# Query-key-normed attention with a gated MLP on one core: a slot's scores, values and sums in one visit of TensorE's small tiles

## The chip, the cores and the metric

The kernel runs on one NeuronCore of a Trainium2 chip. Its engines are TensorE (PE in the profile; PEld is its weight load), VectorE (DVE), ScalarE (ACT), GpSimd (POOL) and the queue that starts transfers (SP). The metric is the device time of one execution in microseconds (us).

## The reference

Attention with normed queries and keys, then a two-layer MLP whose activation is h - tanh(h). All is float32.

```python
batch, n_heads, seq, head_dim = (8, 12, 448, 64)     # d_model 768, d_ff 2048
q_n, k_n = (rmsnorm(q, g_q), rmsnorm(k, g_k))
scores = scale * np.matmul(q_n, k_n.transpose(0, 1, 3, 2))
attn = np.exp(scores - max) / sum
x = np.matmul(attn, v)            # then (batch * seq, heads * head_dim)
h = x @ w_in
out = (h - np.tanh(h)) @ w_out
```

## The kernel before

**Slots.** The attention is cut into 48 slots: 8 batches by 6 pairs of heads. A slot `s` works on 448 queries and 448 keys of two heads. The keys are cut into three chunks of 128 and a last one of 64. For each chunk `scores` (L438) makes the transposed scores, keys on the partitions and queries along the row, for the two heads in two PSUM banks, and an exponential of ScalarE (L443) for each head reads them and writes `p`. Head 0 sits on partitions 0 to 63 and head 1 on 64 to 127, so its two matmuls use the upper and lower half of TensorE's array at once ("64\*128" in the profile). A float32 matmul is two instructions; the profile counts instructions.

- `last_values` (L477) and `values` (L489) multiply the exponentials by V, in tiles of 32 columns, four side by side.
- `totals` (L510) sums the exponentials over the keys by a matmul with ones, also in tiles of 32 columns, and VectorE takes the reciprocal (L515).
- `divide` (L523) multiplies the values by it on VectorE, and the result is `xT`, the MLP's input. For the upper three pairs of heads of a batch it is followed by four sums on GpSimd (`tt`, L537 to L540).
- `turn` transposes queries and keys two slots ahead (L411, L415). `squares`, `norm` (VectorE L129, L130; GpSimd's power L131) and `norm_q` (L400) make the norms three slots ahead. `add` and `add_last` (L459, L460, L467) add up the exponentials on VectorE, so that `totals` has one matmul to do in place of four.

Scores run one slot ahead: in slot `s` the values of `s` are made from exponentials that slot `s - 1` left, and the scores of `s + 1` are made.

**The MLP as a stream.** The MLP of batch `b - 1` runs beside the attention of batch `b`. It is a Python generator, `mlp`, whose matmuls (L578) use the full 128\*128 array. `run(gap)` takes matmuls from it until their time, counted in a fixed figure per matmul, has reached the sum of the gaps asked for. From the third batch on a slot holds four gaps, and a gap is 14 matmuls, 28 instructions. Both layers use products of seven (a Strassen form): per set the order is 1, 5, 6, 2, 3, 7, 4. The hidden layer has four sets of 42 matmuls, three slots; the projection three sets of 56, three slots. What VectorE, ScalarE and GpSimd do behind each product (`use`, L615 to L659, `store`) is issued where the product ends or one product later (`late["todo"]`). In the hidden layer each set ends with `factors`: two sums on VectorE (L625, L626), one on GpSimd (L627).

**The order.** The order of the program is written by hand, and each engine takes its instructions in that order. A slot before is: scores 0 and 1 of the next slot; a gap; `turn`; a gap; the last chunk's scores; `last_values`, `totals`, `values`, `divide`; scores 2; then `add`, `add_last`, `norm` and `norm_q`, each behind half a gap. So TensorE is twice in a slot on small tiles (a visit): once for scores 0 and 1, once from the last chunk's scores to scores 2.

**PSUM.** Of eight banks, three (`mm`) belong to the MLP and five (`sc`) to the attention, and both are dealt out in turn:

```python
banks = {name: [ps.tile([P, 512], F32, name=f"{name}{i}") for i in range(n)] for name, n in (("sc", 5), ("mm", 3))}
def bank_of(name):
    turns[name] += 1
    return banks[name][turns[name] % len(banks[name])]
```

A slot takes 13 turns of the five: six for scores 0 to 2, two for the last chunk, one for the sums, two for the values, two for `turn`. A matmul into a bank waits until the last reader of the bank's previous content is done.

The first batch's slots (`first_slot`) have no MLP beside them and issue scores 2 of one slot and scores 0 and 1 of the following one with no other TensorE work between.

Of the kernel before, what the change touches and what calls it, by code (L numbers as in the profile page):

```python
# [133 lines left out]
def bounded_path(tc, ctx, q, k, v, moe_w_in, moe_w_out, out, g_col, ident, ones, half_ones, neg_half, early):  # L134
# [22 lines left out]
    NP = H // 2  # L157
# [46 lines left out]
    def load(s, names):  # L204
        b, hp = steps[s]
        for name in names:
            src = {"q": q, "k": k, "v": v}[name]
            if s == 0 and name != "v":
                t = early[name]
            else:  # L210
                shape = [CP, 2, NCH, D] if name == "q" else [P, NCH, 2, D] if name == "k" else [P, 2, NCH, D]
                t = nat.tile(shape, F32, name=f"{name}_nat", bufs=3 if name == "v" else 2)
                fetch(nc, name, t, src[b, 2 * hp : 2 * hp + 2])
            loaded[name, s] = t
# [191 lines left out]
    def turn(s, tk, tq):  # L406

        rr, n = normed.pop(s), early["n"]
        kn = loaded.pop(("k", s))
        for c in range(NCH):  # L410
            nc.tensor.transpose(tk[:, c * P : (c + 1) * P], kn[:, c].rearrange("p h d -> p (h d)"), ident)  # L411
        kT = qkp.tile([P, S], F32, name="kT")
        nc.scalar.mul(kT, tk[:, :S], g_col)
        for c in range(NCH):
            nc.tensor.transpose(  # L415
                tq[:, c * CP : (c + 1) * CP], n[:, c].rearrange("p h d -> p (h d)"), ident[:CP, :CP]
            )
        qT = qkp.tile([P, S], F32, name="qT")
        nc.scalar.copy(out=qT, in_=tq[:, :S])
        turned[s] = rr, kT, qT  # L420

    def sc_bank():
        return bank_of("sc")

    def scores(s, c):

        rr, kT, qT = turned[s]
        halves, keys, n = (1, P, S) if c < KF else (2, KR, HS)
        name, bufs = ("p", 2) if c < 2 else ("p_full", 1) if c < KF else ("p_last", 2)
        if c == 1:  # L430
            p = probs[s, 1] = probs[s, 0]
        else:
            p = probs[s, c] = pp.tile([P, 2, 2 if c < 2 else 1, n], F32, name=name, bufs=bufs)
        tiles = [sc_bank() for _ in range(2)]
        for i in range(halves):
            for h in range(2):
                r = slice(h * D, (h + 1) * D)
                nc.tensor.matmul(  # L438
                    tiles[h][i * keys : (i + 1) * keys, :n], lhsT=kT[r, c * P : c * P + keys],
                    rhs=qT[r, i * n : (i + 1) * n], start=True, stop=True,  # L440
                )
        for h in range(2):
            nc.scalar.activation(  # L443
                p[:, h, c if c < 2 else 0, :], tiles[h][:, :n], AF.Exp, scale=rr[:, 0, 2 * c + h : 2 * c + h + 1]
            )
# [5 lines left out]
    def add(s):  # L451

        if s <= NP + NP // 2:
            sums[s] = []
            return
        t = early["sum"]
        sums[s] = [t]
        p = full(s)
        nc.vector.tensor_tensor(out=t, in0=p[0], in1=p[1], op=ALU.add)  # L459
        nc.vector.tensor_tensor(out=t, in0=t, in1=p[2], op=ALU.add)  # L460
# [8 lines left out]
    def last_values(s, av):  # L469

        v_nat, p = loaded["v", s], probs[s, KF]
        for n in range(2):
            keys = slice(n * KR, (n + 1) * KR)
            for m in range(2):
                for h in range(2):
                    r = (2 * m + h) * BL
                    nc.tensor.matmul(  # L477
                        av[n][r : r + BL, :HS], lhsT=v_nat[keys, h, KF, m * BL : (m + 1) * BL],
                        rhs=p[keys, h, 0], start=True, stop=False,
                    )  # L480

    def values(s, av):
        v_nat, p = loaded.pop(("v", s)), full(s)
        for n in range(2):
            for c in range(KF):
                for m in range(2):
                    for h in range(2):
                        r = (2 * m + h) * BL
                        nc.tensor.matmul(  # L489
                            av[n][r : r + BL, :HS], lhsT=v_nat[:, h, c, m * BL : (m + 1) * BL],  # L490
                            rhs=p[c][:, h, n * HS : (n + 1) * HS], start=False, stop=(c == KF - 1),
                        )
        return av

    def totals(s, dn):

        parts = [t[:, h, n * HS : (n + 1) * HS] for t in sums.get(s, ()) for n in range(2) for h in range(2)]
        parts = [(parts, [ones[:, :BL]] * 2)] if parts else []
        if not sums.pop(s):
            for p in full(s):  # L500
                parts.append(
                    ([p[:, h, n * HS : (n + 1) * HS] for n in range(2) for h in range(2)], [ones[:, :BL]] * 2)
                )
            last = probs[s, KF]
            parts.append(([last[:, h, 0] for _ in range(2) for h in range(2)], [half_ones[:, n] for n in range(2)]))
        for i, (moving, by) in enumerate(parts):
            for n in range(2):
                for h in range(2):
                    r = (2 * n + h) * BL
                    nc.tensor.matmul(  # L510
                        dn[r : r + BL, :HS], lhsT=by[n], rhs=moving[2 * n + h],
                        start=(i == 0), stop=(i == len(parts) - 1),
                    )
        rs = whole[s] = sp.tile([P, HS], F32, name="rs")
        nc.vector.reciprocal(rs, dn[:, :HS])  # L515

    def divide(s, av):
        b, hp = steps[s]
        rs = whole.pop(s)
        x = xT[b, hp] = xp.tile([P, S], F32, name="xT")  # L520
        for n in range(2):
            for m in range(2):
                nc.vector.tensor_tensor(  # L523
                    out=x[m * D : (m + 1) * D, n * HS : (n + 1) * HS],
                    in0=av[n][m * D : (m + 1) * D, :HS], in1=rs[n * D : (n + 1) * D], op=ALU.mult,
                )
        for c in range(NCH):
            del probs[s, c]
        if hp < HC:
            return  # L530
        c = hp - HC
        if c == 0:
            tt[b] = tp.tile([P, 3, HC, HS], F32, name="tt", bufs=1)
        eng = nc.vector if b == 0 and c == HC - 1 else nc.gpsimd
        x11, x12, x21, x22 = (xT[b, r][:, n : n + HS] for r in (c, hp) for n in (0, HS))
        t1, t2, t4 = (tt[b][:, i, c] for i in range(3))
        eng.tensor_tensor(out=t1, in0=x12, in1=x11, op=ALU.subtract)  # L537
        eng.tensor_tensor(out=t2, in0=x22, in1=t1, op=ALU.subtract)  # L538
        eng.tensor_tensor(out=x12, in0=x22, in1=x12, op=ALU.subtract)
        eng.tensor_tensor(out=t4, in0=x21, in1=t2, op=ALU.subtract)  # L540
# [225 lines left out]
    def run(ns):  # L766

        spent[1] += ns
        while spent[0] + 1.0 < spent[1]:
            took = next(stream, None)  # L770
            if took is None:
                return
            spent[0] += took
# [4 lines left out]
    def gap_ns(s):  # L778

        if s < 2 * NP:  # L780
            return H_NS / 12 if s % NP < 3 else 4 * S / ENGINE_NS * CD * CF / 12
        return (H_NS + O_NS) / (4 * NP)

    def has(s):
        return 0 <= s < NS
# [32 lines left out]
        weight(EARLY * (s + 3) // (NP + 2))  # L818
        combine(2)

    def slot(s):
        gap = gap_ns(s)
        if s < 2 * NP:
            totals(s, sc_bank())
        if has(s + 1):
            scores(s + 1, 0)
            scores(s + 1, 1)
        if has(s + 2):
            load(s + 2, "v")
        run(gap)  # L830
        if has(s + 2):
            turn(s + 2, sc_bank(), sc_bank())
        if has(s + 3):
            squares(s + 3)
        if has(s + 4):
            load(s + 4, "qk")
        run(gap)
        if has(s + 1):
            scores(s + 1, KF)
        dn = sc_bank() if s >= 2 * NP else None  # L840
        av = [sc_bank() for _ in range(2)]
        last_values(s, av)
        if s >= 2 * NP:
            totals(s, dn)
        divide(s, values(s, av))
        if has(s + 1):
            scores(s + 1, 2)
        for work, n in ((add, 1), (add_last, 1), (norm, 3), (norm_q, 3)):
            run(gap / 2)
            if has(s + n):  # L850
                work(s + n)

    load(0, "qk")
    load(1, "qk")
    weight_load(0)
# [1 line left out]
    for s in range(-3, NP):  # L857
        first_slot(s)
    for s in range(NP, NS):
        slot(s)  # L860
    run(1e9)


# [343 lines left out]
```

## Time and profile before

Three runs gave 1463.94, 1464.91 and 1466.45 us; the median is 1464.91.

| engine | busy us | share of the span |
|---|---|---|
| TensorE, matmuls | 1429.9 | 98% |
| TensorE, weight loads | 1187.1 | 81% |
| VectorE | 818.6 | 56% |
| GpSimd | 512.0 | 35% |
| ScalarE | 456.7 | 31% |

The MLP's matmuls (L578) make up 64% of the chain that ended last, the scores (L438) 9%, the values (L489) 6%. From the third batch on a slot takes 28.94 us. In the timeline a line gives start, length, engine, source line, operation, output and inputs, shape and count; in brackets stand the idle time before it and what ended it. "issue" there means that no awaited engine is seen.

### The profile page before, as it was taken

The page shows a single profiled execution, that of the slowest core. Times are in us where ns is not written, and L with a number is a line of the kernel's source. Part 1 is how long each engine was busy: PE and PEld are TensorE (multiplying, and loading weights), DVE is VectorE, ACT ScalarE, POOL GpSimd, SP SyncE. Part 2 cuts the span into 40 slices and gives each one's busy share as a digit, 9 for nine tenths or more (in the row PEclk, how much of TensorE's full clock was granted, in tenths as well). Part 3 has the DMA queues.
Part 4 walks back from the last instruction along what each step waited for, and adds up shares of the span by engine and source line. Part 5 has one row for each costly group of instructions (what it writes and reads, how often), then busy time and mean ns, then how long its engine had stood idle before and what let it go on. Part 6 is the DMA issues. An engine that isn't in the chain of part 4 may idle for free.

```text
span 1463.9 us, 26034 instructions
## 1 busy us (share of the span) xinstructions
PE 1429.9 (98%) x10272; PEld 1187.1 (81%) x10272; DVE 818.6 (56%) x1246; ACT 456.7 (31%) x850; POOL 512.0 (35%) x378
## 2 busy tenths in 40 slices
PE   6999899999999999999999999999999999999997
PEld 3568654488888888888888888888888888889997
DVE  4999888755553665347535555555554366433322
ACT  5755443233222332223322233213322233201100
POOL 4656465224321334214422243322433133312310
PEclk9999899999999999999999999999999999999999
DMA  8769778855566545655555555555556654555663
GB/s 184 173 189 267 239 194 224 228 171 154 169 157 173 166 150 157 176 156 154 176 158 164 160 154 176 160 142 172 171 152 164 169 163 139 148 164 162 183 194 98
DMA packets 267895, 250.74 MB, mean 171 GB/s; under 512 B 164724, under 2 KB 210036, under 8 KB 267764
## 3 DMA queue, kind: packets, MB, share of 16 engines
q1 hardware_dynamic: 267760, 248.97, 60.0%
q8 instruction: 84, 1.38, 0.4%
q14 instruction: 47, 0.39, 0.1%
q10 hardware_dynamic: 4, 0.00, 0.0%
HBM read 215.48 MB, written 33.42 MB: 170 GB/s over the span
## 4 chain that ended last, share of the span: by engine, by line
PE 89%; DVE 5%; DMA 2%; SPq 1%; ACT 1%; issue 1%; POOL 0%; ACTq 0%
PE mm L578 64%; PE sc L438 9%; PE sc L489 6%; PE mm L743 4%; PE sc L477 1%; PE sc L510 1%; PE sc L411 1%; PE sc L415 1%; DMA q_nat<-in_q_dram 1%; DVE w_out L82 1%; DVE rs L515 1%; DVE w_out L78 1%; DMA gT<-in_moe_w_in_dram 1%; DVE w_out L79 1%; DVE w_out L320 1%
## 5 line engine op out<-in xcount | busy, mean ns | idle before, releaser
L578 PE MATMUL mm<-xT,w_f 128*128 128x224 f32 x1392 | 278.8, 355 | 0.0
L578 PEld LDWEIGHTS mm<-xT,w_f 128*128 128x128 f32 x1392 | 260.3, 190 | 16.9 <-issue 9.8
L578 PEld LDWEIGHTS mm<-gT,w_f 128*128 128x128 f32 x1344 | 251.4, 190 | 22.5 <-issue 15.3
L578 PE MATMUL mm<-gT,w_f 128*128 128x224 f32 x1344 | 267.7, 355 | 0.0
L131 POOL TENSOR_TENSOR rr<-rr,neg_half 112x8 f32<-112x8 f32 x96 | 156.7, 1651 | 205.1 <-DVE rr L130 203.3
L615 POOL TENSOR_TENSOR gT<-s,th 128x448 f32<-128x448 f32 x96 | 121.2, 1267 | 297.3 <-ACT th L614 296.6
L578 PE MATMUL mm<-tt,w_f 128*128 128x224 f32 x1044 | 211.2, 354 | 0.0
L578 PEld LDWEIGHTS mm<-tt,w_f 128*128 128x128 f32 x1044 | 196.1, 190 | 7.8 <-issue 7.8
L578 PE MATMUL mm<-tg,w_f 128*128 128x224 f32 x1008 | 200.4, 353 | 0.0
L578 PEld LDWEIGHTS mm<-tg,w_f 128*128 128x128 f32 x1008 | 189.5, 190 | 0.0
L438 PE MATMUL sc<-qT,kT 64*128 64x448 f32 (+1 forms) x960 | 172.6, 503 | 12.9 <-ACT p_last L443 9.2
L443 ACT ACTIVATE p<-sc,rr 128x448 f32<-128x448 f32 x192 | 106.1, 638 | 203.2 <-PE sc L438 203.2
L538 POOL TENSOR_TENSOR tt<-xT,tt 128x224 f32<-128x224 f32 x23 | 31.4, 1364 | 290.7 <-DVE xT L523 290.6
L438 PEld LDWEIGHTS sc<-qT,kT 64*128 64x128 f32 (+1 forms) x960 | 62.8, 167 | 81.4 <-issue 62.7
L515 DVE RECIPROCAL rs<-sc 128x224 f32<-128x224 f32 x42 | 65.4, 1557 | 77.5 <-PE sc L510 77.4
L443 ACT ACTIVATE p_full<-sc,rr 128x448 f32<-128x448 f32 x96 | 55.9, 632 | 144.4 <-PE sc L438 144.4
L614 ACT ACTIVATE th<-s 128x448 f32<-128x448 f32 x96 | 55.5, 578 | 101.0 <-DVE s L640 55.9
L489 PE MATMUL sc<-p,v_nat 128*32 128x224 f32 x1344 | 79.1, 353 | 0.0
L743 PE MATMUL mm<-gT,w_out 128*128 128x448 f32 x192 | 76.4, 555 | 0.0
L443 ACT ACTIVATE p_last<-sc,rr 128x224 f32<-128x224 f32 x96 | 37.9, 449 | 114.3 <-PE sc L438 114.3
L697 DVE TENSOR_TENSOR s<-mm,s 128x224 f32<-128x224 f32 x21 | 8.2, 392 | 116.7 <-PE mm L578 109.3
L523 DVE TENSOR_TENSOR xT<-sc,rs 64x224 f32<-64x224 f32 x168 | 65.3, 389 | 10.3 <-PE sc L489 2.3
(123 smaller groups left out, 1632.0 us busy)
## 6 DMA issues: line engine op xcount, KB each, us to landing
w_f<-w_in SPq DMA_DIRECT2D x196, 384.0 KB, 3.5
w_f<-w_out SPq DMA_DIRECT2D x147, 512.0 KB, 4.3
w_raw<-in_moe_w_out_dram SPq DMA_DIRECT2D x16, 768.0 KB, 5.2
out_dram<-th SPq DMA_DIRECT2D x192, 56.0 KB, 2.0
q_nat<-in_q_dram SPq DMA_DIRECT2D x47, 224.0 KB, 4.4
v_nat<-in_v_dram SPq DMA_DIRECT2D x48, 192.0 KB, 3.8
k_nat<-in_k_dram SPq DMA_DIRECT2D x94, 96.0 KB, 2.9
w_in<-w_out SPq DMA_DIRECT2D x21, 384.0 KB, 6.4
```

The costliest lines, as they stand in the source:

```text
L78: nc.vector.tensor_scalar(out=dst, in0=dst, scalar1=HI_MIN, scalar2=HI_MAX, op0=ALU.max, op1=ALU.min)
L131: nc.gpsimd.tensor_tensor(out=r, in0=r, in1=neg_half[:rows], op=ALU.pow)
L438: nc.tensor.matmul(tiles[h][i * keys : (i + 1) * keys, :n], lhsT=kT[r, c * P : c * P + keys], rhs=qT[r, i * n : (i + 1) * n], start=True, ...
L443: nc.scalar.activation(p[:, h, c if c < 2 else 0, :], tiles[h][:, :n], AF.Exp, scale=rr[:, 0, 2 * c + h : 2 * c + h + 1])
L489: nc.tensor.matmul(av[n][r : r + BL, :HS], lhsT=v_nat[:, h, c, m * BL : (m + 1) * BL], rhs=p[c][:, h, n * HS : (n + 1) * HS], start=False, ...
L515: nc.vector.reciprocal(rs, dn[:, :HS])
L523: nc.vector.tensor_tensor(out=x[m * D : (m + 1) * D, n * HS : (n + 1) * HS], in0=av[n][m * D : (m + 1) * D, :HS], in1=rs[n * D : (n + 1) * ...
L538: eng.tensor_tensor(out=t2, in0=x22, in1=t1, op=ALU.subtract)
L578: nc.tensor.matmul(bank[:, f * HS : (f + 1) * HS], lhsT=w[:, c * width + f, :], rhs=moving[p](c), start=(first and f == 0 and c == 0), sto ...
L614: nc.scalar.activation(th, h, AF.Tanh, bias=0.0, scale=1.0)
L615: eng.tensor_tensor(out=g[:, rows, cols], in0=h, in1=th, op=ALU.subtract)
L743: nc.tensor.matmul(bank[:, :S], lhsT=w_out_row(f, n // HC)[:, n % HC * P : (n % HC + 1) * P], rhs=g[:, f, :], start=(f == 0), stop=(f == C ...
```

## The change

From slot 12 on there is one visit in place of two. It begins the slot: the last chunk's scores of the next slot, the sums and values of this one, and then all three full chunks of the next slot's scores. The slot's work on the other engines and the gaps are dealt out anew behind it; the four gaps stay four. `slot` of before becomes `early_slot` and serves the second batch only. The purpose is that TensorE changes over to its small tiles and back once in a slot.

```diff
-    def slot(s):
+    def early_slot(s):
         gap = gap_ns(s)
-        if s < 2 * NP:
-            totals(s, sc_bank())
+        totals(s, sc_bank())
...
-        dn = sc_bank() if s >= 2 * NP else None
         av = [sc_bank() for _ in range(2)]
         last_values(s, av)
-        if s >= 2 * NP:
-            totals(s, dn)
         divide(s, values(s, av))
...
+    def slot(s):
+
+        gap = gap_ns(s)
+        if has(s + 1):
+            scores(s + 1, KF)
+        dn = sc_bank()
+        av = [sc_bank() for _ in range(2)]
+        last_values(s, av)
+        totals(s, dn)
+        divide(s, values(s, av))
+        if has(s + 1):
+            for c in range(KF):
+                scores(s + 1, c)
+        if has(s + 2):
+            load(s + 2, "v")
+        run(gap / 2)
+        if has(s + 1):
+            add(s + 1)
+        run(gap / 2)
+        if has(s + 2):
+            turn(s + 2, sc_bank(), sc_bank())
+        if has(s + 3):
+            squares(s + 3)
+        if has(s + 4):
+            load(s + 4, "qk")
+        for work, n, share in ((add_last, 1, 1), (norm, 3, 0.5), (norm_q, 3, 1)):
+            run(gap * share)
+            if has(s + n):
+                work(s + n)
+        run(gap / 2)
...
-        slot(s)
+        (early_slot if s < 2 * NP else slot)(s)
```

## The prediction

> **What bounds the kernel now.** I read the page first (busy shares, then the chain that ended last), then TensorE's timeline over one slot, then its weight loads at the edges of a visit, then VectorE and ScalarE around the visits.
>
> The page: busy shares, and the chain by engine and line.
>
> ```profile
> PE 1429.9 (98%) x10272; PEld 1187.1 (81%) x10272; DVE 818.6 (56%) x1246; ACT 456.7 (31%) x850; POOL 512.0 (35%) x378
> PE 89%; DVE 5%; DMA 2%; SPq 1%; ACT 1%; issue 1%; POOL 0%; ACTq 0%
> ```
>
> TensorE is the bound, and from the third batch on it has no holes. Four slots, each asked as a window of its own, read alike; two of them:
>
> ```profile
> 321.20:350.14 28.94, 28.94 (x213) 24.91 (x212) 19.05 (x31) 9.39 (x18) 14.12 (x11) 1.00 0.52 154
> 1247.28:1276.22 28.94, 28.94 (x213) 24.91 (x213) 13.85 (x19) 6.38 (x13) 11.78 (x11) 1.00 0.41 116
> ```
>
> The columns are time, then busy time of PE, PEld, DVE, ACT, POOL, the clock and DMA. A slot is 28.94 us, PE is busy for all of it, and nothing in it waits for data. So only what changes TensorE's own sequence can change the time. TensorE's timeline of one slot (start, length, line, tile, count):
>
> ```profile
> 697.42 1.77 PE L438 MATMUL sc<-qT,kT 64*128 64x448 f32 x8
> 699.12 3.29 PE L578 MATMUL mm<-xT,w_f 128*128 128x224 f32 x16
> ...
> 710.75 0.61 PE L438 MATMUL sc<-qT,kT 64*64 64x224 f32 x8
> 711.29 0.61 PE L477 MATMUL sc<-p_last,v_nat 64*32 64x224 f32 x16
> 711.83 0.58 PE L510 MATMUL sc<-rows,ones 128*32 128x224 f32 x8
> 712.23 0.94 PE L489 MATMUL sc<-p,v_nat 128*32 128x224 f32 x16
> ...
> 714.62 1.02 PE L438 MATMUL sc<-qT,kT 64*128 64x448 f32 x4
> 715.57 1.78 PE L578 MATMUL mm<-tt,w_f 128*128 128x224 f32 x8
> 717.19 6.97 PE L578 MATMUL mm<-xT,w_f 128*128 128x224 f32 x36
> 724.00 2.43 PE L578 MATMUL mm<-tt,w_f 128*128 128x224 f32 x12
> 726.36 1.77 PE L438 MATMUL sc<-qT,kT 64*128 64x448 f32 x8
> ```
>
> Two visits of small tiles per slot: one at 697.42 (score chunks 0 and 1 of the next slot, 8 instructions) and one at 710.75 that ends with chunk 2 (4 instructions) at 714.62. Between them run MLP instructions. What an edge between the two kinds costs is in the weight loads of the visit at 726.36:
>
> ```profile
> 726.36 0.30 PEld L438 LDWEIGHTS sc<-qT,kT 64*128 64x128 f32 x4 [0.28 <-issue]
> ...
> 728.06 2.00 PEld L578 LDWEIGHTS mm<-gT,w_f 128*128 128x128 f32 x11 [0.65 <-issue]
> ```
>
> The loads stand idle 0.28 us before the visit and 0.65 us behind it: weights are not loaded ahead across an edge.
>
> **What the Trainium skill says.** "TensorEngine Tiling (Array Packing)", Key Properties: changing the tiling mode drains TensorE. The trace agrees: the idle loads above. The same page, PSUM Bottleneck: tiling speeds up TensorE but not the emptying of PSUM. It agrees too: a pair of score tiles takes TensorE 0.75 us, its two exponentials (L443) take ScalarE 2.21 us for four, 0.55 each, 1.1 a pair. "SBUF — State Buffer", Who interferes with whom: a VectorE instruction with two SBUF inputs contends with GpSimd's reads. It agrees: L625 has 0.63 us alone and 1.54 with a GpSimd subtraction beside it.
>
> **The change, part by part.** It concerns slots 12 to 47. The MLP instructions per slot stay 112 (four gaps of 28, dealt out as 0.5+0.5+1+0.5+1+0.5). All 35 slots with a next one (12 to 46) lose the score visit of their own.
>
> 1. Removed. The visit goes from 697.42 to 699.12: 1.704 us by the trace's start times. Its two edges in the MLP stream go as well: 36 MLP instructions from 717.19 to 724.00 are 0.1892 us each, 56 of them should take 10.595, and from 715.57 to 726.36 they take 10.79: 0.195 for the two edges. Together 1.90 us.
>
> 2. Added. Chunks 0 and 1 join chunk 2 behind the values in the same tile shape, so no edge comes between. A pair more is 1.77 - 1.02 = 0.75 us; two are 1.504 (1.704 - 0.952 per two pairs, doubled). Gross: 1.90 - 1.504 = 0.395 us a slot, 13.8 us over 35.
>
> 3. A new wait. The scores rotate over five PSUM banks. In the new order a slot takes: the last chunk two (a, b), the sums one (c), the values two (d, e), then chunk 0 a and b, chunk 1 c and d, chunk 2 e and a. So chunk 2's second tile needs bank a, which chunk 0's first exponential must have read. Before, the nearest case was chunk 2 behind the last chunk's exponentials, which ended 2.4 us ahead of it. The trace of before has just this: in the first batch, where chunks 2, 0, 1 come in one go of 12 instructions on the same five banks, the sixth tile waits for the first.
>
> ```profile
> 42.02 2.82 PE L438 MATMUL sc<-qT,kT 64*128 64x448 f32 x12
> ...
> 44.77 0.33 PE L411 MATMUL mm<-ident,k_nat 128*128 128x128 f32 x1
> ```
>
> ```profile
> 43.13 1.16 ACT L443 ACTIVATE p_full<-sc,rr 128x448 f32<-128x448 f32 x2 [1.94 <-PE sc L438]
> ```
>
> That visit takes 44.77 - 42.02 = 2.75 us; three pairs without a wait would be 0.952 + 1.504 = 2.456. So the wait costs 0.29. The exponential starts there 1.11 us into the visit and ends 0.64 later; the weight load that waited starts 0.05 behind its end. In the slots in question an exponential starts 1.05 us after its pair (727.41 against 726.36), or 1.11 in two of six slots, so the cost is 0.23 to 0.29. I take 0.25; the ends give the range. Behind the waiting load stands only the rest of the visit and then the MLP, that is, all of TensorE.
>
> 4. Waits for VectorE. Banks c, d and e come free from the reciprocal (L515) and the four products of divide (L523), which were in nobody's way before. From the timeline of VectorE in the slot at 710.75:
>
> ```profile
> 712.54 1.56 DVE L515 RECIPROCAL rs<-sc 128x224 f32<-128x224 f32 x1 [1.74 <-PE sc L510]
> 714.20 1.63 DVE L523 TENSOR_TENSOR xT<-sc,rs 64x224 f32<-64x224 f32 x4
> ```
>
> Counting from the visit's start, c is free at 3.35 us, d (two products) at 4.24, e at 5.08. The weight loads that need them would start at 4.36 (chunk 1) and 5.10 (chunk 2), and may come 0.19 later without loss, as loads run ahead of their matmuls. So c and d are in time, e just, and e's lateness lies under wait 3. VectorE may be some 0.25 us late before this costs anything. Is it? In the new order the visit stands where the old score visit stood in the MLP stream. There VectorE's queue is empty by 1.79 us, when the reciprocal can start, in slots 0, 2, 4 and 5 of a batch, since norm and norm_q stand 14 and 7 MLP matmuls earlier now. In slot 3 (visit at 726.36) the hidden layer's last two factors, L625 and L626, lie directly ahead, and today L625 waits for GpSimd, which is held by L131 until 0.5 us, and runs its slow form. In the new order L131 is done some 5 us earlier. The same spot in the last batch, with no attention beside it, shows how it then goes:
>
> ```profile
> 1392.70 0.62 DVE L648 TENSOR_TENSOR s<-mm,s 128x448 f32<-128x448 f32 x1 [1.11 <-PE mm L578]
> 1393.24 0.62 DVE L625 TENSOR_TENSOR tg<-gT 128x448 f32<-128x448 f32 x1
> 1393.96 0.63 DVE L626 TENSOR_TENSOR tg<-gT,tg 128x448 f32<-128x448 f32 x1
> ```
>
> L648 starts 0.11 us after the visit's start, so L626 ends at 0.11 + 1393.96 + 0.63 - 1392.70 = 2.0 us: the reciprocal is 0.2 late, which costs at most 0.1. Slot 1 has its factors 8 MLP matmuls (3 us) earlier and should be close to this. For the 12 slots together I take off 0.5 us.
>
> 5. Moved, at no cost. The transposes (turn) keep the array's full shape, hence no edge. The loads keep their places in the stream; add and add_last lie under MLP work, add 7 matmuls (2.6 us) behind the visit, when the sixth exponential, 4.3 us after the scores began, is done. A ScalarE copy or tanh behind six exponentials comes some 1.6 us after the visit's end at the latest, as today behind four, and the next product is 6 matmuls (2.3 us). xT comes half a slot earlier, which only gives slack. GpSimd's sums for tt start after a divide and are needed a slot or more later.
>
> Sum: 0.395 - 0.25 = 0.145 us a slot, times 35 = 5.1, less 0.5: 4.6 us. From 1464.9 to 1460.3 us.
>
> **The rivals.**
> - The wait on bank a is hidden: 13.8 us gained, 1451 us. For it: ScalarE is 31% busy. Against: the first batch's visits of 12 show the wait with ScalarE idle before it. Chance 0.08.
> - The waits eat the gain: 0.40 a slot instead of 0.25, from an exponential that starts 0.15 late or from banks d and e: 1465 us. For it: the margin is 0.145 in 28.94, and d and e have only 0.2 us of air. Chance 0.18.
> - Slower: VectorE's factors keep the slow form ahead of the reciprocal. Today L626 ends 3.9 us after the start of the visit at 726.36; the reciprocal would be 2.1 us late and bank d 1.8 us behind the last moment at which it costs nothing; 0.25 of that takes the place of wait 3. About 1.6 us in each of the six slots with number 3 in their batch is 9.6 us, against 5.1 gained: 1469 us; 1479 if slots 1 do the same. For it: the order of GpSimd's queue decides, and I derived it from the program. Against: the last batch. Chance 0.15.
>
> **How the numbers follow.** The forecast has 0.59, the rivals 0.08, 0.18 and 0.15. Forecast with both ends of the bank wait and VectorE's 0 to 1.5 us: 13.8 - 35 x 0.29 - 1.5 = 2.2 gained to 13.8 - 35 x 0.23 = 5.8, so 1459.1 to 1462.7. The range goes from 1455 (part of the bank wait hidden) to 1467 (the second rival and the mildest of the third). Faster by over 0.2% (under 1462.0): 0.08 + 0.58 = 0.66; within: 0.18; slower: 0.16.
>
> **What would show each step.** A slot of 28.8 us instead of 28.94 (forecast), 28.55 (hidden) or more. One group of 12 instructions of L438 in 64*128 tiles per slot, and its length from the first start to the next MLP start: 2.69 to 2.75 us right, 2.46 wrong. 84 MLP instructions in one stretch. A wait of L438's loads for ScalarE's exponential of chunk 0, some 0.2 us, 35 times; a wait for L523 there, above all in slots 3, would mean the third rival. L625 at 0.63 us in slots 3. If some slots exceed 28.94, the sum fails at step 4; if all do, at step 3.

## The result, and the profile after

The first comparison, four runs of each, gave 1456.39 us (1455.29 to 1456.84) against 1464.43 us (1462.94 to 1466.45): a ratio of 0.9943, 95% interval 0.9926 to 0.996, or 8 us less. The same kernel run again beside more runs of the one before (the first experiment) came to 0.9964, 0.995 to 0.9977, or 5.5 us less in the medians. The second figure is the better one, since it rests on more runs; the first experiment shows why the first was too good.

The page of the changed kernel: busy shares, and the chain by engine.

```profile
PE 1422.4 (98%) x10272; PEld 1199.3 (82%) x10272; DVE 812.9 (56%) x1246; ACT 452.9 (31%) x850; POOL 477.9 (33%) x378
PE 92%; DVE 3%; DMA 2%; SPq 2%; ACT 1%; issue 1%; POOL 0%; ACTq 0%
```

TensorE is still the bound and runs as many instructions as before. Single slots of the changed kernel, one early and one late, asked by window (time; busy PE, PEld, DVE, ACT, POOL; clock; DMA):

```profile
404.35:433.12 28.77, 28.77 (x213) 25.30 (x212) 12.71 (x22) 6.83 (x14) 5.75 (x6) 1.00 0.60 169
1238.73:1267.51 28.78, 28.78 (x214) 25.37 (x213) 10.94 (x18) 6.25 (x13) 7.92 (x9) 1.00 0.45 126
```

A slot takes 28.77 us where it took 28.94. TensorE's timeline of the first of them:

```profile
404.35 0.61 PE L438 MATMUL sc<-qT,kT 64*64 64x224 f32 x8
404.89 0.61 PE L477 MATMUL sc<-p_last,v_nat 64*32 64x224 f32 x16
...
408.22 2.76 PE L438 MATMUL sc<-qT,kT 64*128 64x448 f32 x12
410.90 3.29 PE L578 MATMUL mm<-gT,w_f 128*128 128x224 f32 x16
...
417.12 3.96 PE L578 MATMUL mm<-tg,w_f 128*128 128x224 f32 x20
420.92 9.24 PE L578 MATMUL mm<-gT,w_f 128*128 128x224 f32 x48
430.00 3.19 PE L578 MATMUL mm<-tg,w_f 128*128 128x224 f32 x16
433.12 0.42 PE L438 MATMUL sc<-qT,kT 64*64 64x224 f32 x4
```

There is one visit; its 12 instructions of scores last from 408.22 to 410.90, and 84 MLP instructions follow the transposes in one stretch, 417.12 to 433.12. By the trace's start times the 12 take 2.686 us in every slot but the first (2.716), where 2.456 would be the time without a wait (the prediction's step 3). Weight loads and exponentials of the same visit:

```profile
408.21 0.30 PEld L438 LDWEIGHTS sc<-qT,kT 64*128 64x128 f32 x4 [0.36 <-issue]
408.70 0.19 PEld L438 LDWEIGHTS sc<-qT,kT 64*128 64x128 f32 x2 [0.18 <-DVE xT L523]
409.07 0.19 PEld L438 LDWEIGHTS sc<-qT,kT 64*128 64x128 f32 x2 [0.18 <-issue]
409.45 0.19 PEld L438 LDWEIGHTS sc<-qT,kT 64*128 64x128 f32 x1 [0.18 <-DVE xT L523]
409.82 0.42 PEld L438 LDWEIGHTS sc<-qT,kT 64*128 64x128 f32 x3 [0.19 <-issue]
410.90 0.49 PEld L578 LDWEIGHTS mm<-gT,w_f 128*128 128x128 f32 x3 [0.65 <-issue]
```

```profile
409.27 2.21 ACT L443 ACTIVATE p<-sc,rr 128x448 f32<-128x448 f32 x4 [3.45 <-PE sc L438]
```

Loads come in pairs, one for each head, but the fifth stands alone at 409.45 and its partner is in the group of three at 409.82: chunk 2's second tile. Taken singly it starts at 409.954, 0.052 us behind the end of chunk 0's first exponential (start 409.27, length 0.63). That is the wait for bank a. It doesn't show as idle time, since another load is under way. What does show, 0.18 us "until L523", is the usual distance of two loads and costs nothing.

### The profile page after: what moved, and what is told of

It reads as the page before. It is cut to its first block, busy times and chain, and to the rows that moved or that the text cites. A ratio compares the mean times of both kernels' runs of the same rounds, so it can differ in the third digit from the quotient of the medians.

```text
span 1455.0 us, 25920 instructions
## 1 busy us (share of the span) xinstructions
PE 1422.4 (98%) x10272; PEld 1199.3 (82%) x10272; DVE 812.9 (56%) x1246; ACT 452.9 (31%) x850; POOL 477.9 (33%) x378
## 4 chain that ended last, share of the span: by engine, by line
PE 92%; DVE 3%; DMA 2%; SPq 2%; ACT 1%; issue 1%; POOL 0%; ACTq 0%
PE mm L578 65%; PE sc L438 9%; PE sc L489 6%; PE mm L743 4%; PE sc L510 2%; PE sc L477 1%; PE sc L411 1%; PE sc L415 1%; DMA w_raw<-in_moe_w_out_dram 1%; PE mm L489 1%; SPq L261 1%; DVE rs L515 1%; DMA k_nat<-in_k_dram 0%; DMA gT<-in_moe_w_in_dram 0%; SPq L114 0%
## 5 line engine op out<-in xcount | busy, mean ns | idle before, releaser
L131 POOL TENSOR_TENSOR rr<-rr,neg_half 112x8 f32<-112x8 f32 x96 | 156.5, 1649 | 369.5 <-DVE rr L130 367.4
L578 PE MATMUL mm<-gT,w_f 128*128 128x224 f32 x1344 | 263.0, 354 | 0.0
L615 POOL TENSOR_TENSOR gT<-s,th 128x448 f32<-128x448 f32 x96 | 118.0, 1236 | 260.9 <-ACT th L614 260.9
L438 PE MATMUL sc<-qT,kT 64*128 64x448 f32 (+1 forms) x960 | 170.5, 500 | 12.1 <-ACT p_last L443 8.8
L438 PEld LDWEIGHTS sc<-qT,kT 64*128 64x128 f32 (+1 forms) x960 | 73.6, 167 | 83.9 <-issue 49.8
L538 POOL TENSOR_TENSOR tt<-xT,tt 128x224 f32<-128x224 f32 x23 | 17.1, 743 | 186.5 <-DVE xT L523 186.5
L523 DVE TENSOR_TENSOR xT<-sc,rs 64x224 f32<-64x224 f32 x168 | 65.3, 389 | 9.7 <-PE sc L489 2.2
L743 PEld LDWEIGHTS mm<-gT,w_out 128*128 128x128 f32 x192 | 36.4, 193 | 37.3 <-issue 36.3
L459 DVE TENSOR_TENSOR rows<-p 128x896 f32<-128x896 f32 x38 | 42.2, 1111 | 42.0 <-ACT p L443 42.0
```

The lines of the kernel that those rows point to most:

```text
L131: nc.gpsimd.tensor_tensor(out=r, in0=r, in1=neg_half[:rows], op=ALU.pow)
L438: nc.tensor.matmul(tiles[h][i * keys : (i + 1) * keys, :n], lhsT=kT[r, c * P : c * P + keys], rhs=qT[r, i * n : (i + 1) * n], start=True, ...
L523: nc.vector.tensor_tensor(out=x[m * D : (m + 1) * D, n * HS : (n + 1) * HS], in0=av[n][m * D : (m + 1) * D, :HS], in1=rs[n * D : (n + 1) * ...
L578: nc.tensor.matmul(bank[:, f * HS : (f + 1) * HS], lhsT=w[:, c * width + f, :], rhs=moving[p](c), start=(first and f == 0 and c == 0), sto ...
L615: eng.tensor_tensor(out=g[:, rows, cols], in0=h, in1=th, op=ALU.subtract)
L743: nc.tensor.matmul(bank[:, :S], lhsT=w_out_row(f, n // HC)[:, n % HC * P : (n % HC + 1) * P], rhs=g[:, f, :], start=(f == 0), stop=(f == C ...
```

## The experiments

The ratio is to runs of the kernel before that were made beside the kernel in question. "Slot" is the usual slot between 12 and 46; "slot 12 at" is where slot 12 starts in the profile; the last column is from there to the end of the profiled run. Two cells of merged_old_place are empty: there the visit is not what begins a slot.

| kernel | median us (runs) | ratio to before, 95% | slot us | slot 12 at | rest us |
|---|---|---|---|---|---|
| before (first profile) | 1464.43 (4) | | 28.94 | 292.3 | 1171.6 |
| changed (first profile) | 1456.39 (4) | 0.9943 (0.9926 to 0.996) | 28.77 | 289.2 | 1165.8 |
| after_again | 1458.33 (10) | 0.9964 (0.995 to 0.9977) | 28.77 | 287.9 | 1165.7 |
| before_again | 1464.47 (14) | 1.0007 (0.9994 to 1.0019) | 28.94 | 291.5 | 1171.8 |
| merged_old_place | 1457.31 (8) | 0.9958 (0.9941 to 0.9974) | 28.77 | | |
| new_order_apart | 1463.06 (14) | 1.0001 (0.9989 to 1.0013) | 28.94 | 286.6 | 1171.6 |
| three_visits | 1479.61 (4) | 1.0094 (1.0071 to 1.0118) | 29.34 | 293.7 | 1185.8 |
| exp_swapped | 1478.55 (4) | 1.0089 (1.0068 to 1.0111) | 29.34 | 297.3 | 1185.6 |
| late_norms | 1485.87 (4) | 1.0138 (1.0114 to 1.0161) | 28.77; slots 3: 31.7 to 35.0 | 293.0 | 1193.4 |
| chunk0_early | 1460.19 (14) | 0.9961 (0.9949 to 0.9974) | 28.74 to 28.84 | 294.6 | 1165.6 |
| last_chunk_32 | 1451.84 (6) | 0.9914 (0.9897 to 0.9931) | 28.61 | 289.8 | 1160.8 |
| no_wait_32 | 1447.89 (5) | 0.9896 (0.9877 to 0.9914) | 28.41 to 28.52 | 286.9 | 1155.1 |

**Both kernels once more.** No edit.

> The changed kernel once more, unedited. The two profiles differ by 8.9 us, of which 5.9 lie behind slot 12 (35 slots by 0.167) and 3.0 before it, where the two programs are the same. Theory: the change is worth 5.9 us, the rest is the scatter of waits for transfers in the first 290 us, so over more rounds the difference of the medians comes down toward 6 us, and slot 12 starts at another time than 289.2 us. Rival: the change does something to the first 290 us too; then the difference stays near 8 us and slot 12 starts near 289.2 again.

> The kernel before once more, unedited, for a second profile. Theory (scatter ahead of slot 12): slot 12 starts a few us away from the 292.3 us of the first profile in either direction, and from slot 12 to the end it takes 1171.6 us again within 0.3. Rival (systematic): slot 12 starts at 292.3 within 0.5.

Measured: from slot 12 to the end 1165.7 and 1171.8 us, as in the first profiles within 0.2. Where slot 12 starts moves, from 286.6 to 297.3 us over the profiles of the table, though all these programs are alike up to there. So the change is worth 5.9 us, and of the first comparison's 8.9 us between the profiles 3.0 were scatter.

The expected cause, waits for transfers, isn't seen. The largest of them between 60 and 292 us is ScalarE's for weights that come in from memory, and it is 0.8 us shorter in the changed kernel, not 3 (waits by pair: us in total, times, longest; the kernel before, then the changed one):

```profile
ACT w_out L71 <- DMA w_raw<-in_moe_w_out_dram: 27.3, 8, 6.7
ACT w_out L71 <- DMA w_raw<-in_moe_w_out_dram: 26.5, 9, 6.2
```

What does differ is the clock that TensorE was granted, as a share of full speed. It is the third number from the end in these lines, again the kernel before and the changed one:

```profile
0.00:286.00 286.00, 259.71 (x1988) 163.11 (x1989) 237.00 (x334) 149.53 (x253) 148.09 (x98) 0.95 0.79 211
0.00:286.00 286.00, 261.05 (x1996) 162.89 (x1997) 239.54 (x339) 149.40 (x253) 149.01 (x99) 0.98 0.79 214
```

Most of the 3 us arises late in this part: the same TensorE instruction starts at 171.79 and 171.34, another at 198.33 and 197.31, a third at 245.50 and 242.42. Between the last two the kernel before has a stretch at about half clock (0.51 from 198.2 to 201.7), the changed one has 1.00 there. The mean clock is 0.95 and 0.98 in their second profiles too, 0.93 in exp_swapped, where slot 12 starts last, and 0.99 in no_wait_32, where it starts almost first. In single runs it is the same: of the ten of after_again the five from 1455.39 to 1457.12 us have a mean clock of 0.992 to 0.996 over the whole run, the five from 1459.54 to 1460.98 one of 0.989 to 0.991. The four runs recorded on chip 8 (three_visits, exp_swapped, late_norms, chunk0_early) have the four latest starts of slot 12. So the scatter goes with the granted clock; whether the lower clock makes the time, or both come from something else, was not tried. In the slots of both kernels shown above, all from slot 12 on, the clock is 1.00.

**The merging alone, and the order alone.** The first keeps the old order and moves chunks 0 and 1 behind the values:

```diff
-        if has(s + 1):
+        if has(s + 1) and s < 2 * NP:
             scores(s + 1, 0)
             scores(s + 1, 1)
...
-            scores(s + 1, 2)
+            for c in range(0 if s >= 2 * NP else 2, KF):
+                scores(s + 1, c)
```

> The kernel before with chunks 0 and 1 moved behind chunk 2's place, the visit, turn, norms and sums where they stood before. Theory (the saved edges are the gain): a slot takes 28.77 us again, and the gain is the whole one, about 5.9 us against before. Rival (the new deal of the work around the visit brings part of it, or is needed to keep VectorE in time): a slot takes longer than 28.8, or some slots of each batch do.

The second keeps the new order, with chunks 0 and 1 half a gap behind the visit and `add` half a gap behind the transposes:

```diff
-            for c in range(KF):
-                scores(s + 1, c)
+            scores(s + 1, 2)
...
         run(gap / 2)
         if has(s + 1):
-            add(s + 1)
+            scores(s + 1, 0)
+            scores(s + 1, 1)
...
-        for work, n, share in ((add_last, 1, 1), (norm, 3, 0.5), (norm_q, 3, 1)):
+        for work, n, share in ((add, 1, 0.5), (add_last, 1, 0.5), (norm, 3, 0.5), (norm_q, 3, 1)):
```

> The changed kernel's order, but chunks 0 and 1 in a visit of their own half a gap behind the big one. Theory: the edges are back and the wait for the bank is gone, so a slot takes 28.94 us and the time equals that of before within 2 us. Rival (the order, not the merging): the time stays near 1456 us.

Measured: 28.77 us a slot and a ratio of 0.9958 for the merging without the order; 28.94 us and 1.0001 for the order without the merging. A slot of each, the merging alone first:

```profile
302.12:330.89 28.77, 28.77 (x214) 25.30 (x213) 18.26 (x26) 10.01 (x19) 11.59 (x9) 1.00 0.61 181
401.90:430.84 28.94, 28.94 (x214) 24.91 (x213) 12.72 (x22) 6.84 (x14) 5.76 (x6) 1.00 0.62 169
```

The merging is the whole gain; of the two places of the visit in the MLP's stream neither is better, as long as the norms stand where they do in these runs.

**The price of a visit.** One visit more than before:

```diff
             scores(s + 1, 0)
-            scores(s + 1, 1)
+            if s < 2 * NP:
+                scores(s + 1, 1)
...
-        run(gap)
+        run(gap / 2)
+        if has(s + 1) and s >= 2 * NP:
+            scores(s + 1, 1)
+        run(gap / 2)
```

> The kernel before with chunk 1 taken out of chunk 0's visit into a visit of its own half a gap later: three visits a slot. Theory (each visit costs 0.20 us inside and 0.195 at its two edges): a slot takes 28.94 + 0.395 = 29.33 us, in all 13.8 us more than before, about 1478 us. Rival (the cost of a visit is not in its edges but in what it waits for): no more than 2 us longer.

TensorE's timeline:

```profile
440.39 1.02 PE L438 MATMUL sc<-qT,kT 64*128 64x448 f32 x4
441.34 2.92 PE L578 MATMUL mm<-gT,w_f 128*128 128x224 f32 x14
444.19 1.02 PE L438 MATMUL sc<-qT,kT 64*128 64x448 f32 x4
445.14 0.65 PE L578 MATMUL mm<-gT,w_f 128*128 128x224 f32 x2
```

14 MLP instructions take 444.19 - 441.34 = 2.85 us instead of 14 x 0.1892 = 2.65: 0.20 at the edges. A pair alone takes 0.95 instead of 0.75. The slot is 29.34 us, 0.40 more, and the rest of the run 14.2 us longer. The price is met.

**The wait for the bank, made longer.**

```diff
-        for h in range(2):
+        for h in (1, 0) if s > 2 * NP and c == 0 else (0, 1):
             nc.scalar.activation(
```

> The changed kernel with chunk 0's two exponentials in the other order from slot 12 on, so that the bank that chunk 2's second tile needs is read second, 0.53 us later. Theory (that bank is the wait of 0.23 us): the visit's 12 instructions take 2.69 + 0.53 = 3.22 us, a slot 29.30, about 18 us more than the changed kernel. Rival (the 0.23 us are an edge or VectorE's banks): the visit stays at 2.69 and the time at 1456 us.

Weight loads of a visit:

```profile
420.10 0.19 PEld L438 LDWEIGHTS sc<-qT,kT 64*128 64x128 f32 x1 [0.19 <-issue]
420.80 0.29 PEld L438 LDWEIGHTS sc<-qT,kT 64*128 64x128 f32 x2 [0.51 <-ACT p L443]
421.75 1.81 PEld L578 LDWEIGHTS mm<-gT,w_f 128*128 128x128 f32 x10 [0.65 <-issue]
```

Now the wait is long enough to be seen as idle time, and it is ScalarE's. The 12 instructions take 3.25 us and the slot 29.34, 0.57 more for an exponential that comes 0.53 later. So the 0.23 us of the changed kernel are this bank.

**VectorE's air.** The norms at their old places:

```diff
-        for work, n, share in ((add_last, 1, 1), (norm, 3, 0.5), (norm_q, 3, 1)):
+        for work, n, share in ((add_last, 1, 1), (norm, 3, 1.5), (norm_q, 3, 0.5)):
...
-        run(gap / 2)
```

> The changed kernel with norm and norm_q back at their old places in the stream, norm 7 MLP matmuls before the visit and norm_q right before it. Theory (VectorE is in time only because the norms stand earlier): in slots 3 of a batch the reciprocal starts some 3 us late and in slots 1 some 2 us, the visit waits there for L523, and the time is 20 to 30 us above the changed kernel's; slots 0, 2, 4, 5 keep 28.77. Rival (VectorE has air enough): 1456 us as the changed kernel.

VectorE at a visit in slot 3, first the changed kernel (visit from 375.58), then this one (visit from 379.32):

```profile
375.69 0.62 DVE L648 TENSOR_TENSOR s<-mm,s 128x448 f32<-128x448 f32 x1 [1.11 <-PE mm L578]
376.23 0.61 DVE L625 TENSOR_TENSOR tg<-gT 128x448 f32<-128x448 f32 x1
376.95 0.62 DVE L626 TENSOR_TENSOR tg<-gT,tg 128x448 f32<-128x448 f32 x1
377.49 1.55 DVE L515 RECIPROCAL rs<-sc 128x224 f32<-128x224 f32 x1
```

```profile
380.76 1.55 DVE L625 TENSOR_TENSOR tg<-gT 128x448 f32<-128x448 f32 x1 [0.72 <-POOL gT L615]
382.42 0.63 DVE L626 TENSOR_TENSOR tg<-gT,tg 128x448 f32<-128x448 f32 x1
382.96 1.62 DVE L400 TENSOR_TENSOR n<-q_nat,rr 112x512 f32<-112x512 f32 x1
384.51 1.54 DVE L515 RECIPROCAL rs<-sc 128x224 f32<-128x224 f32 x1
```

TensorE at the same place,

```profile
383.18 1.02 PE L438 MATMUL sc<-qT,kT 64*128 64x448 f32 x4
386.11 3.76 PE L438 MATMUL sc<-qT,kT 64*128 64x448 f32 x8 [1.91 <-DVE rs L515]
```

and GpSimd shortly before it:

```profile
376.39 3.24 POOL L131 TENSOR_TENSOR rr<-rr,neg_half 112x8 f32<-112x8 f32 x2 [7.29 <-DVE rr L130]
```

The reciprocal starts 5.2 us after the visit's start instead of 1.9. Of these 3.3 us the factors bring 1.7: L626 ends 3.7 us after the visit's start instead of 2.0, since L131 holds GpSimd until 379.6, L615 comes late and L625 runs in its slow form. The other 1.6 are `norm_q` (L400), which now stands directly ahead of the reciprocal. The run moved both and doesn't tell what one of them alone would cost.

TensorE stands still for 1.91 us there, as in all six slots 3. Behind this stand the granted clock falls. The columns are as in the windows above; first a part of the slot shown, then another of the six slots as a whole:

```profile
387.60:391.00 3.40, 3.40 (x9) 1.79 (x8) 1.35 (x3) 2.09 (x5) 2.76 (x3) 0.50 0.02 5
1088.15:1119.87 31.72, 29.81 (x213) 25.19 (x212) 15.64 (x23) 7.64 (x15) 12.33 (x11) 1.00 0.45 131
```

The second of these slots is the only one of the six with the full clock throughout, and it is 2.95 us longer than 28.77. Four of the six slots have one stretch of 3.4 us at half clock and are 4.5 to 4.6 us longer, one has 6.8 us of it and is 6.2 longer. The six add up to 27.4 us. As an estimate from these numbers, 6 x 2.95 = 17.7 of them are the wait for VectorE and the other 10 the lower clock behind it. Why it fell in five slots of the six the trace doesn't show.

I had expected slots 1 to lose 2 us as well; they keep 28.77. There the reciprocal starts 0.3 us late, which costs nothing. So the third rival was real, and the new places of the norms are what keeps it away.

**Without the wait for the bank, at the price of a change of shape.**

```diff
             scores(s + 1, KF)
+            scores(s + 1, 0)
...
-            for c in range(KF):
+            for c in range(1, KF):
```

> The changed kernel with chunk 0's scores between the last chunk's and last_values, so that their exponentials run while the values are made and no bank is waited for, at the price of one more change of tile shape inside the visit. Theory: the change of shape costs 0.20, the wait saves 0.23, and last_values may wait 0.1 for the last chunk's second exponential: a slot of 28.74 to 28.84 us, within 3 us of the changed kernel. Rival (a change between two small shapes costs nothing, only that from and to the full array): 28.54, 8 us less.

Measured: 28.74 to 28.84 us, the same rest within 0.2 us. By start times chunk 0's pair takes 0.95 us there in place of 0.75, and the visit's last eight instructions of scores 1.70, their time without a wait. So this change between two small shapes costs 0.20 us, about what the wait cost.

**The last chunk in the shape of its neighbour.**

```diff
+                for o in range(0, keys, BL if c == KF and s > 2 * NP else keys):
+                    w = BL if c == KF and s > 2 * NP else keys
                     nc.tensor.matmul(
-                    tiles[h][i * keys : (i + 1) * keys, :n], lhsT=kT[r, c * P : c * P + keys],
+                        tiles[h][i * keys + o : i * keys + o + w, :n], lhsT=kT[r, c * P + o : c * P + o + w],
```

> The changed kernel with the last chunk's scores in tiles of 64*32 in place of 64*64 from slot 13's scores on (16 instructions for 8), so that they have the shape of last_values, which follow. Theory (each change of tile shape inside the visit costs some 0.1 us, as the step from the last start of one shape to the first of the next is 0.28 against 0.19 within one): a slot loses about 0.1 us, 28.67 in place of 28.77, 3.5 us in all. Rival (only the changes from and to the full array cost): 28.77 again, or more because of twice the instructions.

Measured: 28.61 us, 0.16 less than the changed kernel and more than the 0.1 expected. TensorE's timeline (the lines are numbered 2 higher here):

```profile
404.45 0.61 PE L440 MATMUL sc<-qT,kT 64*32 64x224 f32 x16
404.85 0.58 PE L479 MATMUL sc<-p_last,v_nat 64*32 64x224 f32 x16
405.37 0.59 PE L512 MATMUL sc<-rows,ones 128*32 128x224 f32 x8
```

By start times the last chunk's scores take 0.40 us instead of 0.54, and `last_values` 0.515 instead of 0.54. A rival is that the narrower tiles are faster by themselves. Each of the two groups runs in two rounds, and their single starts bound that: 0.11 us are saved at the step from the last chunk's second round to `last_values` (0.19 instead of 0.30), 0.025 at the step between the two rounds of `last_values`, whose shape is the same in both kernels, and only 0.03 between the last chunk's own rounds (0.21 instead of 0.24). The rest of the run is 5.0 us shorter.

**Both together.** Beside the edit above, now for `c in (0, KF)`:

```diff
         tiles = [sc_bank() for _ in range(2)]
+        if c == 2 and s > 2 * NP:
+            tiles[1] = sc_bank()
...
             scores(s + 1, KF)
+            scores(s + 1, 0)
+        av = [sc_bank() for _ in range(2)]
         dn = sc_bank()
-        av = [sc_bank() for _ in range(2)]
...
-            for c in range(KF):
+            for c in range(1, KF):
```

> The changed kernel with the last chunk's and chunk 0's scores in tiles of 64*32, chunk 0 between the last chunk and last_values, the values' banks taken before the sums' bank, and one turn of the banks left out so that chunk 2's second tile gets the sums' bank. Theory (an edge is a change of shape, and the wait is chunk 2's for chunk 0's exponential): no change of shape is added and no bank is waited for, so a slot takes the 28.61 us of the run with the last chunk in 64*32 less 0.23, that is 28.38, and the visit's last 8 instructions of scores take 1.70. Rival (8 tiles of 64*32 with rows of 448 take longer than 2 of 64*128, or a bank of the values is now waited for): 28.6 or more.

TensorE's timeline of a visit (the lines are numbered 4 higher here):

```profile
400.65 1.36 PE L442 MATMUL sc<-qT,kT 64*32 64x224 f32 x32
401.80 0.64 PE L481 MATMUL sc<-p_last,v_nat 64*32 64x224 f32 x16
402.37 0.58 PE L514 MATMUL sc<-rows,ones 128*32 128x224 f32 x8
...
405.16 1.77 PE L442 MATMUL sc<-qT,kT 64*128 64x448 f32 x8
406.86 0.65 PE L582 MATMUL mm<-gT,w_f 128*128 128x224 f32 x2
```

The last eight take 406.86 - 405.16 = 1.70 us: no bank is waited for. A slot takes 28.41 to 28.52, not 28.38: `last_values` take 0.54 to 0.65 us by start times instead of 0.515. Their second bank is now the one that the last chunk's first exponential reads, and in almost every slot their fifth instruction, the first into that bank, starts 0.05 us behind the end of this exponential. That is the same sign as in the wait for bank a, so one bank is still waited for, for a shorter time. The rest of the run is 16.5 us shorter than before and 10.7 shorter than in the changed kernel, and the ratio, 0.9896, is below both kernels.

## Why the prediction was right, point by point

- **Step 1, what is removed:** met. 84 MLP instructions stand in one stretch, and the slot with one visit more is 0.40 us longer, the reverse of the 0.395 of steps 1 and 2. The Trainium skill, "TensorEngine Tiling (Array Packing)", Key Properties, says that a change of tiling mode drains TensorE; these runs give the change a size, 0.20 us inside the visit and 0.20 at its two edges.
- **Step 2, what is added:** met. Where nothing is waited for, two pairs take 1.704 us behind an edge, as before.
- **Step 3, the wait for bank a:** there, and at its lower end: 2.686 - 2.456 = 0.23 us in all slots but the first, where I took 0.25. Swapping two exponentials lengthened it as reckoned.
- **Step 4, VectorE:** mis-sized. I took off 0.5 us; the profile shows 0.03, in the first slot alone, where VectorE's L673 and L400 stand directly ahead of the reciprocal. In slots 3 L625 ran in 0.61 us and the reciprocal started 1.9 us after the visit's start, within its air.
- **Step 5, moved at no cost:** met; PE is busy 28.77 of 28.77 us.
- **The sum:** 35 x (0.395 - 0.23) = 5.8 us against the 4.6 predicted; the profiles show 5.9 from slot 12 on, and the longer comparison 5.5 in the medians. The terms that were off are step 3 by 0.7 us and step 4 by 0.5. The 8 us of the first comparison hold scatter from ahead of slot 12, which the change doesn't touch. Its 1456.39 us lies below the 1459.1 to 1462.7 that the terms gave; the wider range takes it in only because it reached down to 1455 for a bank wait that is hidden in part, and none was hidden. That much of the hit is luck. The interval of the longer comparison, about 3.4 to 7.3 us less, holds the 4.6 as well as the 5.9.
- **A sign that was badly chosen:** I wrote that a wait for L523 in the visit would mean the third rival. The profile lists 64 such gaps, and but for the 0.03 us in the first slot they cost nothing. These are lines of the view of L438 by source in the changed kernel, us and times:

```profile
  issue: 49.8, 185
  ACT p_last L443: 20.2, 7
  DVE xT L523: 13.5, 64
```

Taken singly, 44 of the 64 are 0.18 or 0.19 us, the usual distance of two loads, with the last semaphore's name on it; the others are longer, but outside the first slot the visit took its 2.686 us all the same. Only start times against the pace of 0.376 us told a wait from a gap.

The rivals: the hidden wait (1451 us) and the eaten gain (1465 us) fell by the visit's 2.69 us; the slower one fell because the norms stand earlier: GpSimd's power (L131) is done in time and `norm_q` (L400) is out of the reciprocal's way. It comes true when they stand late.

## What to carry to other kernels

On an engine with no idle time, count its changes of tile shape: between the full array and small tiles a visit cost 0.40 us here, and a change between two small shapes 0.14 to 0.2. Merging two visits saves that, but here it put two tiles of one bank closer together than the bank's reader allowed, so list the turns of the banks and look for the tile whose bank was given out last in the same visit. And place the work of the side engines so that what empties these banks finds its queue empty; here norms that stood 14 and 7 matmuls later cost over 27 us. Part of such a loss can be a lower granted clock behind the wait and not the wait itself, so read the clock of the stretch before you price the wait.

## What the runs showed that I had not expected

Tiles of half the width were the cheaper choice: 16 instructions of 64\*32 in place of 8 of 64\*64 saved 0.16 us a slot, for the greater part since the neighbour has that shape. 32 of them, two chunks at once, took 1.155 us by start times, which is what 0.40 and 0.75 add up to; so four tiles of 32 columns carried 448 columns of queries as fast as one of 128.

Programs that are alike in their first 290 us spread over 10.7 us there, and the spread goes with the granted clock. With four runs of each, a third of the first difference between the profiles was of this kind; comparing from a point where the programs begin to differ gave the size of the change within 0.2 us from a single profile of each.
